# Emitting the engines' programs straight into the main block instead of into a Block

One fused kernel (linear attention plus a gated feed-forward layer) had each engine's instruction stream wrapped in a `Block`. The change writes the five streams directly into the program's main block. What that does to the time is the subject here.

## Chip, cores and metric

The kernel runs on 1 core of one Trainium2 chip. The metric is device time of one execution in microseconds (us). Each execution gives two numbers: its *time*, and its *span*, which runs from the first to the last recorded instruction. The time is longer than the span by about 2 us; that difference I call *time minus span*. All executions quoted are at a granted matrix-engine clock of 0.999 to 1.000. Spans of single executions are known to 0.1 us.

## The reference

```python
def reference(A_x, A_wqkv, A_wo, B_x, B_w_gate, B_w_up, B_w_down):
    x = A_x                                  # [1, 2048, 512], bf16
    xn = _layernorm(x, axis=-1)
    return x + _A_ref(xn, A_wqkv, A_wo) + _B_ref(xn, B_w_gate, B_w_up, B_w_down)
    # _A_ref: linear attention, 32 heads of 16; _B_ref: silu(x@wg)*(x@wu) @ wd, F = 1792
```

The result leaves in 17 output stores, the last of them is issued after the last matmuls (at 211.342 us in the trace of the kernel before, the last matmul record ending at 210.852), and the program waits at its end until it has landed.

## The kernel before

The kernel collects its operations in a list, with their dependences, and then writes each engine's own list out. A wait on another engine or on a transfer is a wait on a semaphore.

```python
    def emit(self, eng_name, eng, sems):
        for o in self.ops:
            if o["eng"] != eng_name:
                continue
            for s, v in o["waits"].items():
                eng.wait_ge(sems[s], v)
            ins = None
            for fn in o["fns"]:
                ins = fn(eng)
            if o["inc"]:
                ins.then_inc(sems[o["sem"]], 16 if o["dma"] else 1)
# ... cut ...
        def oout(bank, t, lo, hi):
            K.add("dve", lambda e: e.tensor_tensor(
                out=out_sb[:, t % 2, lo:hi], in0=banks[bank][:, 0:hi - lo], in1=x_sb[:, t, lo:hi], op=ALU.add),
                r=[B(bank)] + xk(t), w=[("ob", t % 2, lo)])
            K.add("sp", lambda e: e.dma_start(oview[t * P:(t + 1) * P, lo:hi], out_sb[:, t % 2, lo:hi]),
                  r=[("ob", t % 2, lo)], w=[("out", t, lo)], dma=True)
# ... cut ...
        # the last operation of all: SyncE waits until every output store has landed
        K.add("sp", [], r=[("out", t, 0) for t in range(NT)] + [("out", 15, h)])

        K.number()
        sems = {("eng", e): E(nc.semaphore("s_" + e)) for e in ("pe", "act", "dve", "pool", "sp")}
        for i in range(K.ndma):
            sems[("dma", i)] = E(nc.semaphore("d%d" % i))

        with nc.Block() as block:

            @block.sync
            def _(eng):
                K.emit("sp", nc.sync, sems)
            # ... the same for gpsimd, tensor, scalar and vector ...
```

A Block gives each engine a body of its own, with a branch into it and a branch out of it: ten in the program as it is written. At its end stands an all-engine barrier, a meeting point of all five engines. As the trace of the kernel before shows it, each engine drains (VectorE's drain, for one, ends at 211.367 us, after its last work at 211.315) and reports, GpSimd gathers the four reports (213.076) and releases everybody (213.154).

Of the kernel before, what the change touches and what calls it, by code (L numbers as in the profile page):

```python
# [105 lines left out]
def bass_parallel_sum__linear_attn_block__swiglu_ffn__prompt_kernel(nc, A_x, A_wqkv, A_wo, B_x, B_w_gate, B_w_up, B_w_down, out):  # L106
    xin = A_x[0]
    oview = out[0]
    K = _Program()
    bf, f32 = dt.bfloat16, dt.float32  # L110

    with contextlib.ExitStack() as es:
# [423 lines left out]
        sems = {("eng", e): E(nc.semaphore("s_" + e)) for e in ("pe", "act", "dve", "pool", "sp")}  # L536
        for i in range(K.ndma):
            sems[("dma", i)] = E(nc.semaphore("d%d" % i))

        with nc.Block() as block:  # L540

            @block.sync
            def _(eng):
                K.emit("sp", nc.sync, sems)

            @block.gpsimd
            def _(eng):
                K.emit("pool", nc.gpsimd, sems)

            @block.tensor  # L550
            def _(eng):
                K.emit("pe", nc.tensor, sems)

            @block.scalar
            def _(eng):
                K.emit("act", nc.scalar, sems)

            @block.vector
            def _(eng):
                K.emit("dve", nc.vector, sems)  # L560


# [26 lines left out]
```

## Time and profile before

| | before |
|---|---|
| time, median of 3 | 215.41 us (215.18 to 215.76) |
| span of the profiled execution | 213.3 us |
| PE (matrix engine) busy | 208.3 us, 98% of the span |
| end of SyncE's wait for the last store (its exit branch), to the end of the span | 0.34 us |

The page of the kernel before, its first lines and the chain of work that ended last (shares of the span by engine):

```profile
span 213.3 us, 2668 instructions
PE 208.3 (98%) x991; PEld 95.5 (45%) x991; DVE 126.4 (59%) x217; ACT 69.8 (33%) x138; POOL 55.5 (26%) x81
...
PE 89%; DVE 5%; ACT 2%; DMA 1%; issue 1%; SPq 0%; DVEq 0%
```

The kernel is bound by PE nearly from end to end. The change adds and takes nothing there (991 weight loads in both traces).

What it does touch are instructions that the page does not count as busy. They appear when one asks for everything that belongs to the Block's own source line, 540 (engine, operation, count: shortest/median/longest duration in ns, first and last start in us; a trailing "q" is that engine's sequencer, whose records here are waits, branches and drains):

```profile
L540 POOLq EVENT_SEMAPHORE  x2: 17/17/17, 213.1 to 213.2; - x2
L540 POOLq DRAIN  x1: 1267/1267/1267, 131.5 to 131.5; - x1
L540 ACTq DRAIN  x1: 627/627/627, 190.6 to 190.6; - x1
L540 PEldq DRAIN  x1: 2155/2155/2155, 208.7 to 208.7; - x1
L540 DVEq DRAIN  x1: 464/464/464, 210.9 to 210.9; - x1
L540 SPq COMPARE_BRANCH  x1: 33/33/33, 212.9 to 212.9; - x1
L540 SPq DRAIN  x1: 7/7/7, 213.0 to 213.0; - x1
L540 SPq EVENT_SEMAPHORE  x1: 17/17/17, 213.2 to 213.2; - x1
L540 ACTq EVENT_SEMAPHORE  x1: 17/17/17, 213.2 to 213.2; - x1
L540 DVEq EVENT_SEMAPHORE  x1: 21/21/21, 213.2 to 213.2; - x1
L540 PEldq EVENT_SEMAPHORE  x1: 51/51/51, 213.2 to 213.2; - x1
```

The long drains of GpSimd, ScalarE, PE and VectorE end by 211.4 us (at 132.787, 191.189, 210.898 and 211.367), long before SyncE's own drain starts at 213.043, so they are free. Only SyncE's own drain and what follows it can cost anything. And there is one branch in the whole trace (2668 records), not ten: the COMPARE_BRANCH that carries SyncE's wait.

SyncE's waits, from the view of the waits of the transfer queue (in total us, times, longest), name what it stood on:

```profile
SPq L540 <- DMA out_dram<-out_sb: 1.1, 1, 1.1
...
SPq L540 <- PEq L540: 0.2, 1, 0.2
```

First it waits 1.1 us for the last store, then 0.2 us for the barrier. Read record by record from the packed trace (no view prints these lines), the same end is this (start in us, duration in ns, sequencer, operation):

```
211.342  332  SyncE    DMA_DIRECT2D     the last output store is issued
211.725   28  SyncE    EVENT_SEMAPHORE  waits for the two stores before it
212.886   33  SyncE    COMPARE_BRANCH   waits for the last store; the Block's exit
213.043    7  SyncE    DRAIN
213.076   17  GpSimd   EVENT_SEMAPHORE  gathers
213.154   17  GpSimd   EVENT_SEMAPHORE  releases
213.196   17  SyncE    EVENT_SEMAPHORE  takes the release (ScalarE 213.201, VectorE 213.207)
213.207   51  PE       EVENT_SEMAPHORE  takes the release: the span ends at 213.258
```

The trace also notes when a transfer lands: the last store at 212.869 us.

At the start of the program stands another barrier, recorded from 0 to 0.78 us, which belongs to the launch (line 574). The timeline there (start us, length us, engine, line, operation):

```profile
0.80 1.28 ACT L183 ACT_TABLE_LOAD   x1 [0.80 <-PEq L574]
0.80 0.10 POOL L196 MEMSET eps<- 128x1 f32 x1 [0.29 <-POOLq L574]
0.80 0.86 SPq L157 DMA_DIRECT2D x_sb<-in_A_x_dram  x2
```

ScalarE, GpSimd and SyncE start their own work at 0.80 us and PE at 0.81; VectorE starts at 2.95, after a wait of 3.0 us for a load of x (the view of the waits).

### The profile page before, as it was taken

The page shows a single profiled execution, that of the slowest core. Times are in us where ns is not written, and L with a number is a line of the kernel's source. Part 1 is how long each engine was busy: PE and PEld are TensorE (multiplying, and loading weights), DVE is VectorE, ACT ScalarE, POOL GpSimd, SP SyncE. Part 2 cuts the span into 40 slices and gives each one's busy share as a digit, 9 for nine tenths or more (in the row PEclk, how much of TensorE's full clock was granted, in tenths as well). Part 3 has the DMA queues.
Part 4 walks back from the last instruction along what each step waited for, and adds up shares of the span by engine and source line. Part 5 has one row for each costly group of instructions (what it writes and reads, how often), then busy time and mean ns, then how long its engine had stood idle before and what let it go on. Part 6 is the DMA issues. An engine that isn't in the chain of part 4 may idle for free.

```text
span 213.3 us, 2668 instructions
## 1 busy us (share of the span) xinstructions
PE 208.3 (98%) x991; PEld 95.5 (45%) x991; DVE 126.4 (59%) x217; ACT 69.8 (33%) x138; POOL 55.5 (26%) x81
## 2 busy tenths in 40 slices
PE   7999999999989999999999999999999999999995
PEld 2444444444434444444444444444444444444454
DVE  3899985546967999594677776663233223241121
ACT  3797975546553333122131313021123122130000
POOL 3257664559934332131222222000000000000000
DMA  6942332499900212112102020201000000000001
GB/s 193 352 104 49 71 67 58 129 379 375 353 21 0 52 25 49 47 27 52 25 25 49 26 52 25 49 25 49 3 25 0 25 0 29 0 25 23 26 28 49
DMA packets 26765, 15.78 MB, mean 74 GB/s; under 512 B 16512, under 2 KB 26752, under 8 KB 26752
## 3 DMA queue, kind: packets, MB, share of 16 engines
q1 hardware_dynamic: 25920, 14.88, 24.6%
q10 hardware_dynamic: 832, 0.72, 1.0%
q8 instruction: 8, 0.13, 0.3%
q14 instruction: 5, 0.04, 0.1%
HBM read 9.70 MB, written 2.10 MB: 55 GB/s over the span
## 4 chain that ended last, share of the span: by engine, by line
PE 89%; DVE 5%; ACT 2%; DMA 1%; issue 1%; SPq 0%; DVEq 0%
PE pb L382 41%; PE pb L465 23%; PE pb L295 13%; PE pb L319 6%; PE pb L461 6%; DVE zacc L332 2%; DVE hT L395 1%; DMA x_sb<-in_A_x_dram 1%; ACT L390 1%; ACT GT L402 1%; DVE stats L226 0%; DVE zb L419 0%; ACT sil L390 0%; ACT ef L303 0%; DVE kvT L413 0%
## 5 line engine op out<-in xcount | busy, mean ns | idle before, releaser
L390 ACT ACTIVATE sil<-pb 128x512 bf16<-128x512 f32 x56 | 33.3, 597 | 101.4 <-PE pb L382 100.1
L382 PE MATMUL pb<-xnT,wu 128*128 128x512 bf16 x224 | 57.8, 379 | 0.0
L382 PE MATMUL pb<-xnT,wg 128*128 128x512 bf16 x224 | 57.8, 379 | 0.0
L395 DVE TENSOR_TENSOR hT<-pb,sil 128x512 bf16<-128x512 f32 x56 | 37.6, 685 | 32.1 <-PE pb L382 30.4
L465 PE MATMUL pb<-wd,hT 128*128 128x512 bf16 (+1 forms) x238 | 51.2, 366 | 0.0
L465 PEld LDWEIGHTS pb<-wd,hT 128*128 128x128 bf16 x238 | 23.3, 98 | 25.1
L471 DVE TENSOR_TENSOR out_sb<-pb,x_sb 128x512 bf16<-128x512 f32 (+1 forms) x17 | 11.2, 660 | 37.7 <-PE pb L465 37.7
L382 PEld LDWEIGHTS pb<-xnT,wu 128*128 128x128 bf16 x224 | 21.7, 98 | 26.3 <-DVE hT L395 1.1
L382 PEld LDWEIGHTS pb<-xnT,wg 128*128 128x128 bf16 x224 | 21.9, 98 | 25.7
L432 POOL TENSOR_TENSOR pz<-pq,zbc 128x512 f32<-128x512 bf16 x16 | 18.5, 1161 | 55.0 <-DVE den L437 51.4
L295 PE MATMUL pb<-wqkv,xnT 128*128 128x512 bf16 x128 | 29.6, 379 | 0.1
L307 POOL TENSOR_SCALAR ef<-ef 128x512 bf16<-128x512 bf16 x32 | 19.4, 612 | 19.2 <-ACT ef L303 19.0
L303 ACT ACTIVATE ef<-pb 128x512 bf16<-128x512 f32 x32 | 18.3, 591 | 9.4 <-PE pb L295 9.2
L295 PEld LDWEIGHTS pb<-wqkv,xnT 128*128 128x128 bf16 x128 | 12.3, 98 | 15.1 <-ACT xnT L274 0.7
L444 DVE TENSOR_TENSOR pq<-pq,rden 128x512 bf16<-128x512 bf16 x16 | 17.5, 1091 | 0.6
L461 PE MATMUL pb<-M,pk 128*128 128x512 bf16 (+1 forms) x68 | 16.6, 366 | 0.0
L319 PE MATMUL pb<-pk,xn 128*128 128x512 bf16 x64 | 15.4, 379 | 0.0
L314 DVE SCALAR_TENSOR_TENSOR pk<-pb,ef 128x512 bf16<-128x512 f32 x16 | 10.8, 679 | 4.8 <-POOL ef L307 4.8
L314 DVE SCALAR_TENSOR_TENSOR pq<-pb,ef 128x512 bf16<-128x512 f32 x16 | 10.7, 682 | 3.9 <-POOL ef L307 3.9
L226 DVE BATCH_NORM_STATS2 stats<-x_sb 128x6 f32<-128x512 bf16 x16 | 10.9, 679 | 3.3 <-DMA x_sb<-in_A_x_dram 3.3
L437 DVE TENSOR_REDUCE den<-pz 128x32 f32<-128x512 f32 x16 | 10.8, 672 | 0.0
L332 POOL TENSOR_TENSOR zacc<-zacc,pk 128x512 f32<-128x512 f32 x8 | 10.2, 1277 | 0.6
(46 smaller groups left out, 78.1 us busy)
## 6 DMA issues: line engine op xcount, KB each, us to landing
out_dram<-out_sb SPq DMA_DIRECT2D x15, 128.0 KB, 1.7
x_sb<-in_A_x_dram SPq DMA_DIRECT2D x14, 128.0 KB, 4.2
wg<-in_B_w_gate_dram SPq DMA_DIRECT2D x2, 896.0 KB, 7.8
wu<-in_B_w_up_dram SPq DMA_DIRECT2D x2, 896.0 KB, 9.2
wd<-in_B_w_down_dram SPq DMA_DIRECT2D x2, 896.0 KB, 13.8
wqkv<-in_A_wqkv_dram ACTq DMA_DIRECT2D x2, 256.0 KB, 4.0
wqkv<-in_A_wqkv_dram SPq DMA_DIRECT2D x2, 256.0 KB, 4.6
wqkv<-in_A_wqkv_dram SPq DMA_DIRECT2D x1, 512.0 KB, 7.9
```

What stands on the lines that cost most here:

```text
L295: K.add("pe", [(lambda e, c=c: e.matmul(banks[b][:, :], xnT[:, c, t * P:(t + 1) * P], wqkv[:, c, col:col + D], start=(c == 0), stop=(c == ...
L303: K.add("act", lambda e: e.activation(ef[:, b - 4, :], banks[b][:, :], ACT.Exp), r=[B(b)], w=[("ef", b - 4)])
L307: K.add("pool", lambda e: e.tensor_scalar(out=buf, in0=buf, scalar1=1.0 + 1e-6, scalar2=0.0, op0=ALU.min, op1=ALU.max), r=[bkey], w=[bkey])
L314: K.add("dve", lambda e: e.scalar_tensor_tensor(out=dst, in0=banks[b][:, :], scalar=1e-6, in1=ef[:, b - 4, :], op0=ALU.max, op1=ALU.add), ...
L319: K.add("pe", [(lambda e, c=c: e.matmul(banks[c][:, :], xn[:, t, c * P:(c + 1) * P], pk[:, t, :], start=(t == 0), stop=(t == NT - 1))) for ...
L382: fns.append(lambda e, c=c, b=b, w_=w_: e.matmul(banks[b][:, :], w_[:, c, fc * P:(fc + 1) * P], xnT[:, c, C * 512:(C + 1) * 512], start=(c ...
L390: K.add("act", lambda e: e.activation(sil[:, j % 2, :], banks[gb(j)][:, :], ACT.Silu), r=[B(gb(j))], w=[("sil", j % 2)])
L395: K.add("dve", lambda e: e.tensor_tensor(out=hT[:, C % 2, fc, :], in0=banks[gb(j) + 1][:, :], in1=sil[:, j % 2, :], op=ALU.mult), r=[B(gb( ...
L432: K.add("pool", lambda e: e.tensor_tensor(out=pz[:, t % 2, :], in0=pq[:, t, :], in1=zbc[:, :], op=ALU.mult), r=[("pq", t), ("zbc",)], w=[( ...
L444: K.add("dve", lambda e: e.tensor_tensor(out=heads(pq[:, t, :]), in0=heads(pq[:, t, :]), in1=rden[:, i, :][:, :, None].broadcast_to([P, NH ...
L461: fns = [(lambda e, g=g: e.matmul(banks[bank][:, 0:hi - lo], pk[:, t, g * P:(g + 1) * P], M[:, g, lo:hi], start=(g == 0), stop=False)) for ...
L465: fns = [(lambda e, fc=fc: e.matmul(banks[bank][:, 0:hi - lo], hT[:, C % 2, fc, jj * P:(jj + 1) * P], wd[:, fc, lo:hi], start=False, stop= ...
```

## The change

The intent was to drop what the Block adds around the programs: a branch for each engine at its entry and the all-engine barrier at its exit. The order of work and all waits stay as they were.

```diff
-        with nc.Block() as block:
-
-            @block.sync
-            def _(eng):
-                K.emit("sp", nc.sync, sems)
-            ... (cut: the same for gpsimd, tensor, scalar, vector)
+        for name, eng in (("sp", nc.sync), ("act", nc.scalar), ("pe", nc.tensor), ("dve", nc.vector), ("pool", nc.gpsimd)):
+            K.emit(name, eng, sems)
```

More of the change, by code (lines that the diff above doesn't have):

```diff
@@ L538, in bass_parallel_sum__linear_attn_block__swiglu_ffn__prompt_kernel @@
             sems[("dma", i)] = E(nc.semaphore("d%d" % i))
-        with nc.Block() as block:
-            @block.sync
-            def _(eng):
-                K.emit("sp", nc.sync, sems)
-            @block.gpsimd
-            def _(eng):
-                K.emit("pool", nc.gpsimd, sems)
-            @block.tensor
-            def _(eng):
-                K.emit("pe", nc.tensor, sems)
-            @block.scalar
-            def _(eng):
-                K.emit("act", nc.scalar, sems)
-            @block.vector
-            def _(eng):
-                K.emit("dve", nc.vector, sems)
+        for name, eng in (("sp", nc.sync), ("act", nc.scalar), ("pe", nc.tensor), ("dve", nc.vector), ("pool", nc.gpsimd)):
+            K.emit(name, eng, sems)
 _INS = ['A_x', 'A_wqkv', 'A_wo', 'B_x', 'B_w_gate', 'B_w_up', 'B_w_down']
```

## The prediction

> **What bounds the kernel now.** The matrix engine: PE is busy 208.3 us of a 213.3 us span (98%, the page), and PE makes up 89% of the chain that ended last. The granted clock was 1.000. The change touches none of that: the instruction order of the two kernels shows the same work with the same waits on every engine; only a branch at each engine's head, one at its tail, and the exit barrier are gone.
>
> **What is removed, at the trace's durations** (sequencer records, shown by the view of one source line):
>
> - *Entry.* The program-start barrier (0 to 0.74 us) belongs to the launch, not the Block, and stays. No branch is recorded behind it on any engine: SyncE's release ends at 0.737 us and its first load issues at 0.803; ScalarE 0.742 to 0.797. These 55 to 66 ns are about what neighbouring sequencer instructions are apart anyway (GpSimd's two barrier semaphores: 79 ns start to start). [...]
> - *Exit.* The final output store issues at 211.34 and lands about 212.88. SyncE's wait for it sits on its exit branch (212.886, 33 ns; the only branch recorded in the trace). Then, in series: its drain (213.043), the gather on GpSimd (213.076), the release (213.154), the last release taken, ending at 213.258. That is 213.258 - 212.919 = 0.34 us after the last byte. The other engines' drains (VectorE's ends latest, about 211.37) finish before SyncE arrives and cost nothing. Without the Block the wait becomes a plain semaphore wait (17 to 28 ns).
>
> So the span should fall by 0.34 us [...]: from 213.26 to about 212.9 us.
>
> **From span to time.** 215.41 - 213.26 = 2.15 us lie outside the span. [...] SyncE stays last, so I expect 0 to 0.3 us from this.
>
> **Predicted:** 215.41 - 0.36 = 215.05 us, 8 in 10 between 214.5 and 215.5: 0.2% faster, inside the run-to-run spread (215.18 to 215.76), far from 2% (4.3 us). Chances: faster by over 2% 0.01, within 2% 0.98, slower by over 2% 0.01.
>
> **What would show each step.** No branch record at all. The first load still issues 0.75 to 0.80 us into the span. The span ends about 30 ns after SyncE's wait on the last store begins to clear, with no drain, gather or release behind it. PE stays busy 208.3 +- 0.5 us; the final store still takes about 1.5 us to land.
>
> **What would make it wrong.** (a) The 2.15 us outside react: [...] the time falls by up to 1 us. (b) [...] the time stays at 215.4. [...] (d) Noise of 0.2 us in a median of three hides everything.

Passages that rested on nothing that a trace or a run of this case shows are cut from this text, at the marks. The sum was 215.41 - 0.36 = 215.05 us. Of the 0.36 us, 0.34 are the exit, at the trace's durations; the rest, about 0.02 us, was for the entry. Without it the span still comes to 213.26 - 0.34 = 212.92 us. Cut as well are the reasons given for 0 to 0.3 us outside the span and for the outcomes (a) and (b), and the outcome (c). The 0 to 0.3 us and the "up to 1 us" of (a) entered no sum; they were estimates, with no measured number behind them.

## The result, and the profile after

The ratios here are those of the comparison program, for fast runs of the same rounds. They are not quite the ratio of the medians that are quoted, and not every listed execution seems to enter them (the 0.9982 of e12_after below comes out only without its profiled execution of 214.16 us).

| | before | after |
|---|---|---|
| time, median of 4 each | 215.30 us | 214.62 us (214.20 to 215.16) |
| ratio of the fast runs, 95% interval | | 0.9963 (0.9940 to 0.9986) |
| span of the profiled execution | 213.3 us | 212.9 us |
| last store landed, to the end of the span | 0.389 us | 0.023 us |

The interval excludes 1, so there is a gain; it is far from 2%. The page of the kernel after, the same lines as before:

```profile
span 212.9 us, 2638 instructions
PE 208.2 (98%) x972; PEld 96.0 (45%) x991; DVE 126.5 (59%) x217; ACT 69.9 (33%) x138; POOL 55.6 (26%) x81
...
PE 92%; DVE 4%; ACT 2%; issue 1%; DVEq 0%
```

PE is as busy as it was (972 records against 991: some matmul records are missing from this trace, while all 991 weight loads are there). The Block's line is gone. SyncE's final wait is now a wait of its own, on the line that emits waits, 98, and nothing stands behind it:

```profile
L98 SPq EVENT_SEMAPHORE  x2: 17/558/1099, 211.8 to 211.8; - x2
```

In the view of the transfer queue's waits this line takes the place of both lines shown before:

```profile
SPq L98 <- DMA out_dram<-out_sb: 1.1, 1, 1.1
```

Read record by record, as before (start in us, duration in ns):

```
211.380   332  SyncE    DMA_DIRECT2D     the last output store is issued
211.763    17  SyncE    EVENT_SEMAPHORE
211.827  1099  SyncE    EVENT_SEMAPHORE  waits for the last store: the span ends at 212.926
```

The stretch from the issue of the last store to the end of the span went from 213.258 - 211.342 = 1.92 us to 212.926 - 211.380 = 1.55 us: 0.37 us less. The two repetitions have the same stretches in their traces (1.91 us in e1_control, 1.55 in e2_after and e12_after). This stretch is a better measure than the whole span, because spans of the same kernel differ by up to 0.9 us from execution to execution (213.1 to 214.0 in eleven runs of the kernel before), more than the effect.

The start is unchanged, as the timeline shows:

```profile
0.80 1.28 ACT L183 ACT_TABLE_LOAD   x1 [0.80 <-PEq L555]
0.80 0.10 POOL L196 MEMSET eps<- 128x1 f32 x1 [0.29 <-POOLq L555]
0.81 0.87 SPq L157 DMA_DIRECT2D x_sb<-in_A_x_dram  x2
```

SyncE's first load starts at 0.805 us against 0.803, ScalarE's table load at 0.796 against 0.797. No cost of an entry shows, to within 2 ns; no entry branch was left in the compiled program.

What did not fit was the part outside the span. The four runs after had a time minus span of 1.25 to 1.66 us; the kernel before was predicted from 2.15 us (a median time less a profiled span). So the gain looked larger than the 0.34 us that the trace explains, by an amount that four runs could not separate from noise. The experiments are about that amount.

### The profile page after: what moved, and what is told of

Its sections match the earlier page's. It is cut to its first block, busy times and chain, and to the rows that moved or that the text cites. A ratio compares the mean times of both kernels' runs of the same rounds, so it can differ in the third digit from the quotient of the medians.

```text
span 212.9 us, 2638 instructions
## 1 busy us (share of the span) xinstructions
PE 208.2 (98%) x972; PEld 96.0 (45%) x991; DVE 126.5 (59%) x217; ACT 69.9 (33%) x138; POOL 55.6 (26%) x81
## 4 chain that ended last, share of the span: by engine, by line
PE 92%; DVE 4%; ACT 2%; issue 1%; DVEq 0%
PE pb L382 40%; PE pb L465 23%; PE pb L295 12%; PE pb L319 7%; PE pb L461 7%; PE pb L216 2%; DVE zacc L332 2%; DVE hT L395 1%; ACT L390 1%; ACT GT L402 1%; PE pb L267 0%; DVE zb L419 0%; ACT sil L390 0%; ACT ef L303 0%; DVE kvT L413 0%
```

## The experiments

Theory 1 was that the exit barrier's recorded 0.34 us is the whole effect. Theory 2 was that, in addition, work that closes the execution after the last record gets shorter, because four engines now reach it early instead of together with SyncE (in the trace of the kernel after, the last records of GpSimd, ScalarE, PE and VectorE end at 132.8, 191.2, 210.9 and 211.4 us). Such closing work was the author's guess, here and in the expectations below: no record shows it, and the runs can test only what time minus span does. Twelve runs were made, three of them repetitions without an edit, all correct, five rounds each; those of one group ran on the same chip. "Time minus span" is the mean, with lowest and highest.

| run | last wait, and what else | ratio to before (95%) | median us | mean span | time minus span |
|---|---|---|---|---|---|
| before, group 1 | | | 215.14 | 213.42 | 1.88 (1.81 to 1.96) |
| e1_control | the kernel before | 0.9998 (0.9982 to 1.0014) | 215.13 | 213.35 | 1.87 (1.70 to 1.93) |
| e2_after | the kernel after | 0.9972 (0.9958 to 0.9986) | 214.70 | 213.02 | 1.64 (1.55 to 1.75) |
| e3_barrier | after + 1 barrier | 0.9992 (0.9976 to 1.0009) | 215.05 | 213.27 | 1.87 (1.72 to 1.95) |
| e4_together | after, all engines held | 0.9994 (0.9980 to 1.0008) | 215.16 | 213.02 | 2.12 (1.92 to 2.19) |
| before, group 2 | | | 215.15 | 213.34 | 1.82 (1.72 to 1.95) |
| e5_drain_together | as e4, drained first | 1.0000 (0.9986 to 1.0013) | 215.26 | 213.06 | 2.04 (1.98 to 2.16) |
| e6_barrier4 | after + 4 barriers | 1.0068 (1.0055 to 1.0081) | 216.69 | 214.82 | 1.75 (1.68 to 1.81) |
| e7_wait_pool | GpSimd waits, not SyncE | 1.0010 (0.9996 to 1.0023) | 215.25 | 213.24 | 2.06 (2.02 to 2.12) |
| e8_hold_pool | SyncE and GpSimd wait | 0.9999 (0.9986 to 1.0012) | 215.00 | 213.04 | 2.06 (1.93 to 2.20) |
| before, group 3 | | | 214.97 | 213.23 | 1.79 (1.69 to 1.87) |
| e9_wait_act | ScalarE waits, not SyncE | 0.9985 (0.9972 to 0.9999) | 214.63 | 212.98 | 1.71 (1.68 to 1.73) |
| e10_wait_dve | VectorE waits, not SyncE | 0.9981 (0.9968 to 0.9993) | 214.65 | 212.94 | 1.66 (1.61 to 1.72) |
| e11_wait_pe | PE waits, not SyncE | 0.9985 (0.9973 to 0.9998) | 214.72 | 212.86 | 1.84 (1.77 to 1.91) |
| e12_after | the kernel after | 0.9982 (0.9968 to 0.9995) | 214.52 | 212.96 | 1.56 (1.26 to 1.80) |

The time itself is known to about 0.14% (0.3 us) in such a comparison. Time minus span scatters much less in most rows, because what makes spans differ from run to run is in both numbers and cancels. It is the instrument that decides most of what follows.

The kernel after is the exception. Its 14 executions (4 of the result, 5 each of e2 and e12) fall into two groups: four at 1.25 to 1.32 us, ten at 1.55 to 1.80, nothing between. Two of the four belong to the result and two to e12, none to e2. What separates them no run shows. The mean of e12, 1.56, is therefore poorly known: against the kernel before in the same rounds it is 0.23 us less, with a 95% interval of +-0.31 worked out from the listed executions, where e2 has 0.24 +- 0.10.

### e1_control: is the outside part stable?

No edit.

> The kernel before, unchanged, against itself. All theories: ratio 1.000 with an interval of about +-0.002. It gives the spans of single executions before: I expect a spread of about 0.5 us (213.1 to 213.7) and 2.0 us (+-0.2) of time outside the span. If the outside part is also anywhere between 1.3 and 2.1 here, the extra gain seen outside the span is noise.

Measured: ratio 0.9998. Over 17 executions (6 of this run and 11 of its comparison) time minus span stayed within 1.70 and 1.96 us, while the spans ran from 213.1 to 214.0. So the 2.15 us of the prediction was too large (it came from a time and a span of different executions), and the outside part is steady enough to compare.

### e2_after and e12_after: is the extra gain real?

No edit; the kernel after, on two chips.

> The changed kernel, unchanged, again. Theory 1 (exit barrier only, 0.34 us inside the span): ratio 0.9984, time lower by 0.3 to 0.4 us. Theory 2 (the same, and the closing work outside the span gets shorter since four engines arrive early): ratio 0.995 to 0.997, time lower by 0.7 to 1.0 us, with time minus span at 1.3 to 1.6 us against about 2.0 us in the control.

> The changed kernel, unchanged, for comparison on the same chip as e9 to e11: ratio 0.997 (0.996 to 0.999), time minus span 1.5 to 1.7 us, the span 0.35 us shorter than before.

Measured: ratios 0.9972 and 0.9982. Time minus span was 1.64 us against 1.88 of the kernel before in the same rounds, and 1.56 against 1.79: 0.24 and 0.23 us less. The mean spans differed by 0.40 and 0.27 us, around the 0.34 to 0.37 us of the records. Theory 1 alone fails, on e2 (e12 agrees, but is not clear of its own scatter): about a quarter of a microsecond comes from outside the span. The time fell by less than the 0.7 to 1.0 us that I had given for theory 2: differences of the means are 0.24 + 0.40 = 0.64 us and 0.23 + 0.27 = 0.50 us.

### e3_barrier: the barrier alone, without Block

```diff
             K.emit(name, eng, sems)
+        nc.all_engine_barrier()
```

> The changed kernel with one all-engine barrier put back at its end, and no Block: no branches at entry or exit. If the barrier is the whole effect (theories 1 and 2), the time is that of the kernel before, ratio 1.000 (0.999 to 1.001), and the span about 0.1 us shorter than before (no branch between the last wait and the drain). If the entry branches or the placement of the instructions matter (rival), it keeps part of the gain: ratio below 0.998.

Measured: ratio 0.9992, time minus span 1.87 us like the kernel before. In the trace, SyncE's wait ends at 213.242 us and its drain starts at 213.293, 0.051 us later; with the Block's branch in between it was 0.124 us (212.919 to 213.043), and 0.121 us in the control. That gap leaves out the branch's own record. Counted from the landing of the last store, the drain starts 0.174 us later before (0.171 in the control), and 0.073 us later here (0.074 in e6). So the exit branch costs 0.10 us and the bare barrier 213.519 - 213.242 = 0.28 us; together they make up about the 0.37 us. The barrier put back takes the outside gain away in full. For the time, the interval of +-0.17% is too wide to show the 0.10 us of the branch; that figure rests on the records alone.

### e4_together: no barrier, but nobody early

```diff
             K.emit(name, eng, sems)
+            if name != "sp":
+                for i in (K.ndma - 3, K.ndma - 2, K.ndma - 1):
+                    eng.wait_ge(sems[("dma", i)], 16)
```

> The changed kernel, without a barrier, but every other engine waits at its end for the last three output stores too, so all five finish together, as after a barrier, within 0.1 us of SyncE. Theory 1: same as the changed kernel, ratio 0.998. Theory 2 (early arrival shortens the closing work): the part inside the span stays (0.3 us) but time minus span returns to about 2.0 us, ratio about 0.998 against 0.996 for the changed kernel in the same rounds. If time minus span stays at 1.3 to 1.6 us, early arrival is not the reason.

Measured: ratio 0.9994, not the 0.998 that both theories gave. The barrier is gone from the records; the four other engines now end with these two waits each (the view of line 544):

```profile
L544 ACTq EVENT_SEMAPHORE  x2: 17/28/38, 211.0 to 212.9; - x2
L544 POOLq EVENT_SEMAPHORE  x2: 17/30/42, 211.0 to 212.9; - x2
L544 DVEq EVENT_SEMAPHORE  x2: 21/36/50, 211.0 to 212.9; - x2
L544 PEldq EVENT_SEMAPHORE  x2: 51/51/51, 211.0 to 212.9; - x2
```

All five engines end within 0.06 us of each other, and the span is as short as in the kernel after (mean 213.02 in both). Yet the time is that of the kernel before: time minus span rose to 2.12 us, 0.48 us above the kernel after. A shorter span was paid back outside it. The time is 0.48 us above e2's of the same rounds (means). So removing the barrier shows no gain by itself here (the interval still allows 0.2%); the gain is there only when some engine may end early (time minus span 1.64 us in e2, 2.12 here). Which one, and why is 2.12 us even more than the 1.88 us with a barrier?

### e5_drain_together: were it the drains?

```diff
             if name != "sp":
+                eng.drain()
                 for i in (K.ndma - 3, K.ndma - 2, K.ndma - 1):
```

> As e4 (all five engines end together on the last stores, no barrier), with a drain on each of the four other engines just before it starts to wait, which is free there as the drains of the barrier are. Question: why time minus span was 2.12 us in e4, more than the 1.88 us of the control with its barrier. Theory A (the closing work drains each engine, and the barrier's early drains had already paid for that): time minus span falls to about 1.9 us and the time is 0.2 to 0.3 us below e4, ratio 0.998. Theory B (only when an engine reaches its end matters): same as e4, time minus span 2.1 us, ratio 0.9995.

Measured: 2.04 us against 1.82 of the kernel before in the same rounds, ratio 1.0000. The excess over a barrier (0.22 us here, 0.24 in e4) did not go away. Theory A fell, within the scatter of about 0.1 us: it is not that the barrier's early drains had saved draining later.

### e6_barrier4: is a barrier worth what its records say?

```diff
             K.emit(name, eng, sems)
+        for _ in range(4):
+            nc.all_engine_barrier()
```

> The changed kernel with four all-engine barriers at its end. Every theory in which a barrier costs what its records show: each barrier beyond the first adds about 0.25 to 0.5 us to the span and to the time (drain, gather, release; GpSimd's drain may be on the path now), time minus span stays at 1.87 us as with one barrier, so the time is 0.8 to 1.5 us above the kernel before, ratio 1.004 to 1.007. If barriers hide in the closing work, the time moves less than the span.

Measured: ratio 1.0068, that is 0.0068 x 215.15 = 1.5 us above the kernel before; the mean span grew by 1.48 us and time minus span stayed at 1.75. Further barriers cost in time what they show in the span. From release to release on PE they took 0.33, 0.75 and 0.33 us; the middle one was held by SyncE, whose third drain started 0.46 us after its release, for a reason that the trace does not show. The sequence on SyncE and GpSimd is all there in the view of line 543, with SyncE's longest drain 131 ns:

```profile
L543 POOLq EVENT_SEMAPHORE  x8: 17/17/17, 213.0 to 214.5; - x8
...
L543 SPq DRAIN  x4: 7/7/131, 212.9 to 214.3; - x4
```

### e7_wait_pool and e8_hold_pool: is it GpSimd?

In e7 the final wait moves from SyncE to GpSimd; in e8 SyncE keeps it and GpSimd waits as well, while PE, ScalarE and VectorE end early.

```diff
# e7
-        K.add("sp", [], r=[("out", t, 0) for t in range(NT)] + [("out", 15, h)])
+        K.add("pool", [], r=[("out", t, 0) for t in range(NT)] + [("out", 15, h)])
# e8
             K.emit(name, eng, sems)
+            if name == "pool":
+                for i in (K.ndma - 3, K.ndma - 2, K.ndma - 1):
+                    eng.wait_ge(sems[("dma", i)], 16)
```

> The changed kernel with the wait for the output stores on GpSimd in place of SyncE, so SyncE ends about 1.1 us early and GpSimd is last. If only the number of early engines counts, it equals the changed kernel: time minus span 1.64 us, ratio 0.997. If it matters which engine is last [...], time minus span moves by more than 0.15 us: longer if GpSimd's part is the longer one, shorter if SyncE's is.

> The changed kernel, with GpSimd alone held to the end beside SyncE (it waits for the last stores too); VectorE, ScalarE and PE still end early. If GpSimd's share of the closing work is what early arrival hides, time minus span is that of e4, 2.1 us, ratio 0.999 to 1.000. If another engine's is, it stays at 1.64 us, ratio 0.997. In between: more than one contributes.

Measured: 2.06 us in both, as much as in e4 and e5 with all engines held, and the ratios are 1.0010 and 0.9999. The line of waits in e7 shows GpSimd standing there for 1.9 us at the end, and SyncE no more:

```profile
L98 POOLq EVENT_SEMAPHORE  x5: 17/17/1902, 18.9 to 211.3; - x5
```

In e8 the other three engines stay free, and the added line has GpSimd alone (line 544):

```profile
L544 POOLq EVENT_SEMAPHORE  x2: 17/30/43, 211.0 to 212.9; - x2
```

So holding GpSimd alone is enough to lose the whole gain, as far as these intervals show, whether or not SyncE is held too. Two readings were left, both guesses about a stretch without records. Theory P: after its last instruction each engine has closing work of its own, and GpSimd's is the longest. Rival Q: SyncE is the exception, and any other engine that waits for the last store is slow.

### e9_wait_act, e10_wait_dve, e11_wait_pe: the other three

```diff
-        K.add("sp", [], r=[("out", t, 0) for t in range(NT)] + [("out", 15, h)])
+        K.add("act", [], r=[("out", t, 0) for t in range(NT)] + [("out", 15, h)])   # "dve" in e10, "pe" in e11
```

> The changed kernel with the final wait on ScalarE alone; SyncE ends at its last issue, GpSimd at 131 us. Theory P (each engine has its own closing work after its end, and GpSimd's is the longest, about 2.06 us in e7 and e8 against SyncE's 1.64): time minus span is ScalarE's own length, below 2.0 us, and the time is like the changed kernel or better, ratio 0.996 to 0.998. Rival Q (SyncE alone is short, or a wait on an output store is slow on every engine but SyncE): 2.0 to 2.1 us, ratio 0.999 to 1.001 as in e7.

> The same with the final wait on VectorE alone. Theory P: time minus span below 2.0 us, ratio 0.996 to 0.998. Rival Q: 2.0 to 2.1 us, ratio 0.999 to 1.001.

> The same with the final wait on PE alone. Theory P: time minus span below 2.0 us, ratio 0.996 to 0.998. Rival Q: 2.0 to 2.1 us, ratio 0.999 to 1.001. [...]

Measured: 1.71 us with ScalarE last, 1.66 with VectorE, 1.84 with PE. The final wait stands where the edit put it (line 98 in e9, e10 and e11):

```profile
L98 ACTq EVENT_SEMAPHORE  x55: 17/17/1904, 2.8 to 211.0; - x55
L98 DVEq EVENT_SEMAPHORE  x74: 21/21/1901, 2.9 to 211.2; - x74
L98 PEldq EVENT_SEMAPHORE  x20: 51/51/1861, 1.6 to 211.2; - x20
```

All three are faster than the kernel before (the intervals just exclude 1). Whether SyncE is better than VectorE or ScalarE these rounds do not show: its mean is 1.56, but single executions run from 1.26 to 1.80. Rival Q fell: none of the three comes near 2.06. But PE's 1.84 is no less than the 1.79 of the kernel before in the same rounds, so with PE held, too, nothing is gained outside the span; its faster time comes from the span (212.86 against 213.23). What an execution takes outside its span thus differs with the engine that was last:

| last engine | SyncE | VectorE | ScalarE | PE | GpSimd |
|---|---|---|---|---|---|
| time minus span, us | 1.56 and 1.64 (single: 1.26 to 1.80) | 1.66 | 1.71 | 1.84 | 2.06 |

GpSimd above PE, and PE above VectorE and ScalarE, is clear of the scatter (GpSimd's was measured on another chip). The order of the first three is not.

The trace has no records there, so what the engines do in this time was not seen, and closing work of each engine, as theory P has it, was not shown; that the differences arise after the last recorded instruction is inferred from the edits, which changed only the ends of the programs.

## Why the prediction was right or wrong

The time, 214.62 us, lay in the predicted range (214.5 to 215.5) and the class (within 2%) was right. The predicted time itself, 215.05, was 0.43 us too high, and that the median fell inside the range was partly luck: two of the four executions (214.20 and 214.25) lie below it, both with the short time minus span of 1.3 us; the repetitions gave 214.70 and 214.52. Point by point:

- *PE bounds the kernel and is untouched*: right. 208.3 us busy before, 208.2 after.
- *Entry*: no branch is recorded there, as the prediction said, and nothing was gained: SyncE's and ScalarE's first instructions moved by 2 ns at most. The small term that the sum still held for it (about 0.02 us) was not needed.
- *Exit, 0.34 us of the span*: right, and slightly small. From the issue of the last store the span's end moved by 0.37 us: about 0.28 for the barrier and 0.10 for the branch in front of it (from e3). The prediction counted from the end of the branch record and so left about 0.03 us of the branch out. The store itself took the same time (1.527 and 1.523 us from issue to landing), and no branch record is left.
- *Outside the span, "SyncE stays last, so I expect 0 to 0.3 us from this"*: the stated limits held (0.24 and 0.23 us measured), but the predicted time counted none of it (its 0.36 is the 0.34 of the exit and the term for the entry). This is the term of the sum that was mis-sized. With the measured 0.24 us the sum would have been 0.34 + 0.24 = 0.58 us, and the two repetitions gave 0.64 and 0.50 us in means.
- *The reason given with it* was not shown by any trace or run. What the runs show is that it is not the number of early engines (four end early in e7, and nothing is gained: ratio 1.0010): which engine stays matters. Holding GpSimd is enough to lose the gain (time minus span 2.06 us in e7 and e8), and holding PE is enough to lose the part outside the span (1.84 us in e11, 1.79 before).
- *The drain, gather and release come in series after the last byte, so that their removal is worth 0.34 us*: true in the trace, incomplete for the time. e4 removes the same records and shows no gain (ratio 0.9994). The author's reading is that the 0.34 us is earned only because GpSimd's last instruction moves from the exit barrier (213.171 us) to the middle of the kernel (its last record ends at 132.8 us). Why an early end of GpSimd should shorten the time was not shown; nothing of it is in a record. With GpSimd held, the outcome (b), a time that stays, is what happens: the gain is given back outside the span (ratios 0.9994 to 1.0010 in e4, e5, e7 and e8, time minus span 2.04 to 2.12 us).

What lies outside the span no run shows, since nothing is recorded there; 1.56 to 2.12 us in the means is all there is of it, the part before the first record included.

One thing stays open. With GpSimd held on the last store, time minus span is 2.04 to 2.12 us. In the kernel before, GpSimd's last record (the release) ends at 213.171 us, 0.09 us before the span does, so the time after it is 1.82 + 0.09 to 1.88 + 0.09, about 1.91 to 1.97 us. That is 0.13 to 0.16 us less than in the held kernels of the same groups, and e5 showed that the missing drains are not the cause. PE is a rival for the kernel before: its record is the last there, and e11 with PE alone last has 1.84 us, no different from the 1.79 to 1.88 of the kernel before. Which of the two sets the outside part before was not separated (a barrier that leaves GpSimd or PE out would do it). The cause stays open.

## What to carry to other kernels

A barrier at the end of a program is worth asking about, but count it twice: what its records take after the last store (here 0.28 us, 0.37 with the branch), and which engines it holds back from their own end. Let the final wait for the output stand on one engine, and let GpSimd and PE run out early: here SyncE, VectorE and ScalarE served about equally well (time minus span 1.56 to 1.71 us, against 1.84 with PE last and 2.06 with GpSimd), and a version that drops the barrier but holds GpSimd was no faster than one with the barrier (ratio 0.9999 in e8). The whole is 0.2 to 0.4% of a 215 us kernel, so it belongs at the end of tuning, and only a quantity with the run-to-run scatter taken out (here time minus span, or the stretch after the last store) shows where it comes from; look at its single values too, not the mean alone.
